# Copies with rows over 4096 bytes issued as two halves, and the first K load issued by ScalarE

## The chip, the cores and the metric

The kernel runs on one core of one Trainium2 chip. The metric is device time in microseconds (us) from a launch to its end. Three runs of the kernel before took 801.07, 794.12 and 801.41 us; the median is 801.07 us.

## The reference

Three stages follow one another, all in float32.

1. Attention with pooled queries: batch 2, 8 heads, 1152 positions, head size 64. Pairs of neighbouring queries are averaged, which leaves 576 per head and batch.
2. A mixture of experts over 1152 tokens of width 512: 8 experts, hidden width 1024, the two best experts of each token.
3. A dense layer with `h * cos(h)`: 512 to 2048 to 512.

```
q_pool = q.reshape(B, H, S // 2, 2, D).mean(axis=3)
scores = q_pool @ k.T / sqrt(D)
x = (softmax(scores) @ v)                       # heads side by side: [1152, 512]
noisy = x @ w_gate + log1p(exp(x @ w_noise)) * noise
out[token] += weight * (relu(x @ w1[e]) @ w2[e])   # for the token's two best e
h = x @ w_in;  result = (h * cos(h)) @ w_out
```

## The kernel before

**Number format.** Products need float32 accuracy, so each operand is split into a rounded high part and the rest. The scores of a head are `hi(q)*hi(k) + hi(q)*lo(k) + lo(q)*hi(k)`. With a head size of 64, two of the three products share one matmul of 128 rows. For that the operands are stacked on the partitions: the tile `q2` (named `q` in the trace) holds hi(q) twice, `l2` (`l`) holds lo(q) twice, `kt` holds hi(k) and lo(k), one above the other, and `kb` and `qd` serve the one query tile of each head that spans both batches.

**Attention.** Heads are worked in pairs: `hp` is the pair, 0 to 3, and `hl` the head in it. Each head has nine tiles of 128 queries, so there are 72 tiles. Tiles 0 to 3 of a head belong to batch 0, tile 4 to both, tiles 5 to 8 to batch 1. In each tile TensorE computes the scores of the next tile (L281), transposes the exponentials of this one (L321), and multiplies earlier ones with V (L359). VectorE takes the maxima, ScalarE the exponentials, GpSimd splits.

**Operands of a pair** are made while the pair before it is worked on. Their order is set by `plan` (L637): at each tile it lists which step is called, and the step's instructions stand in each engine's queue in that order. The steps are these.

- Q is loaded as 64 partitions per batch with 18 rows of 64 floats each: 4608 bytes of a partition are one contiguous row of the transfer (`load_q`, L85; for pair 0 `load_qb`, L197). Pair 1's loads go from SyncE's queue (SP), pairs 2 and 3 from ScalarE's.
- K is loaded likewise, 128 partitions per batch (`load_k`, L99). Its two heads are interleaved in SBUF, so its rows are 256 bytes long. Pair 0's K comes in three parts per batch and head.
- Q is pooled (L91, L202), transposed and split; K is transposed into `st` and split on GpSimd into `sh` and, in place, the low part in `st` (`k_split`, L227 and L228).
- The halves then have to change partitions, which copies from SBUF to SBUF do, all issued by SP, 64 partitions each: `q_asm` (L147, 4864 bytes per row), `l_asm` (L155, 4864), `k_asm` (L238 to L244, 4608, in the order ka high, KB 0, ka low, kb low, kb high, KB 1), and L752 for pair 0. `q_bd` (L163) copies 512-byte rows.

The score matmul of tile 4 of a pair's first head is the first that reads the `kt` of batch 1.

**The start.** SP issues Q of pair 0 and batch 0 for both heads (L680, L681), then K of batch 0 (six transfers), then Q and K of batch 1, V, and Q of pair 1. VectorE pools Q as soon as it lands (L202). ScalarE's first instruction is the load of its function table.

**Transfers and their marks.** Each transfer signals its landing on one of eight semaphores, which go round: an issue waits until the transfer eight before it has landed. SP and ScalarE share the eight.

**After attention** come the routing (L439), the gather of the experts' tokens, the experts (L967, L998) and the dense layer; their weights stream in over SP. The change touches none of that.

Of the kernel before, what the change touches and what calls it, by code (L numbers as in the profile page):

```python
# [9 lines left out]
F32 = mybir.dt.float32  # L10
# [12 lines left out]
def attn_moe_cos_kernel(ctx, tc, q, k, v, w_gate, w_noise, noise, w1, w2, w_in, w_out, out):  # L23
    nc = tc.nc
# [53 lines left out]
    QB1 = 640  # L78
    KT, Q2, QL, V2, QN, QP, KN, VN = {}, {}, {}, {}, {}, {}, {}, {}

    def load_q(hp, hl):
        t = prep.tile([128, 18, 64], F32, name="qn", bufs=2)
        QN[hp, hl] = t
        for b in range(B):
            (nc.sync if hp == 1 else nc.scalar).dma_start(t[b * 64:(b + 1) * 64], q[b, 2 * hp + hl].rearrange("(p r) d -> p r d", r=18))  # L85

    def pool_q(hp, hl):
        if hl == 0:
# [1 line left out]
        t = QN.pop((hp, hl)).rearrange("p (s r) d -> p s r d", r=2)  # L90
        (nc.gpsimd if hp else nc.vector).tensor_tensor(QP[hp][:, :, hl, :], t[:, :, 0, :], t[:, :, 1, :], op=OP.add)  # L91

    def load_k(hp, b, pool=None):
        t = (pool or prep).tile([128, 9, 2, 64], F32, name="kn", bufs=1)
        KN[hp, b] = t
        cs = [slice(0, 9)] if hp else [slice(3 * j, 3 * j + 3) for j in range(3)]
        for c in cs:
            for hl in range(2):
                nc.sync.dma_start(t[:, c, hl, :], k[b, 2 * hp + hl].rearrange("(p c) d -> p c d", c=9)[:, c])  # L99

    def load_v(hp, hl, b):
        t = qk.tile([128, 9, 64], F32, name="vn", bufs=2)
# [39 lines left out]
    def q_asm(hp, hl, bd=True):  # L142
        t = qk.tile([128, 1216], F32R, name="q2", bufs=3)
        QH = QS[hp]
        Q2[hp, hl] = t
        for s in range(2):
            nc.sync.dma_start(t.bitcast(F32)[s * 64:(s + 1) * 64], QH.bitcast(F32)[hl * 64:(hl + 1) * 64])  # L147
        if bd:
            l_asm(hp, hl)
            q_bd(hp, hl)  # L150

    def l_asm(hp, hl):
        t = QL2[hp, hl] = qk.tile([128, 1216], F32R, name="l2", bufs=2)
        for s in range(2):
            nc.sync.dma_start(t.bitcast(F32)[s * 64:(s + 1) * 64], QL[hp].bitcast(F32)[hl * 64:(hl + 1) * 64])  # L155

    KS, KB, QD, kbp = {}, {}, {}, []

    def q_bd(hp, hl):
        t = QD[hp, hl] = kbp[0].tile([128, 128], F32R, name="qd", bufs=2)  # L160
        for b in range(2):
            c0 = 4 * 128 if b == 0 else 4 * 128 - SQ + QB1
            nc.sync.dma_start(t.bitcast(F32)[b * 64:b * 64 + 64], QL[hp].bitcast(F32)[hl * 64:hl * 64 + 64, c0:c0 + 128])  # L163
# [30 lines left out]
    def load_qb(hl, b):  # L194
        if b == 0:
            QN[0, hl] = prep.tile([128, 18, 64], F32, name="qn", bufs=2)
        nc.sync.dma_start(QN[0, hl][b * 64:(b + 1) * 64], q[b, hl].rearrange("(p r) d -> p r d", r=18))  # L197

    def pool_qb(hl, b, eng):
        rs = slice(b * 64, b * 64 + 64)  # L200
# [30 lines left out]
    def k_asm(hp, b):  # L231
        h, r = KS.pop((hp, b))
        ka, kb = (qk.tile([128, S], F32R, name="kt", bufs=5) for _ in range(2))
        hf = h.bitcast(F32)
        if b == 0:
            k_stack(hp)
        rs = slice(b * 64, b * 64 + 64)
        nc.sync.dma_start(ka.bitcast(F32)[0:64], hf[0:64])  # L238
        if hp:
            nc.sync.dma_start(KB[hp, 0].bitcast(F32)[rs], hf[0:64])  # L240
        nc.sync.dma_start(ka.bitcast(F32)[64:128], r[0:64])
        nc.sync.dma_start(kb.bitcast(F32)[0:64], r[64:128])
        nc.sync.dma_start(kb.bitcast(F32)[64:128], hf[64:128])
        nc.sync.dma_start(KB[hp, 1].bitcast(F32)[rs], hf[64:128])  # L244
        KT[hp, 0, b], KT[hp, 1, b] = ka, kb

    def k_stack(hp):
        for hl in range(2):
            KB[hp, hl] = kbp[0].tile([128, S], F32R, name="kb", bufs=2)
# [387 lines left out]
    def plan():  # L637
# [5 lines left out]
        for hp in range(HP):  # L643
# [6 lines left out]
            if hp:  # L650
                m = n0 - 18
                if hp > 1:
                    at(m, load_q, hp, 0)
                    at(m + 1, load_q, hp, 1)
                d = 1 if hp == 1 else 0
                at(m + 1 + d, pool_q, hp, 0)
                at(m + 2 + d, pool_q, hp, 1)
                at(m + 2, load_k, hp, 0)
                for j in range(3):
                    at(m + (3 + 2 * d, 5 + d, 6 + d)[j], q_group, hp, j)  # L660
                at(m + 7 + d, q_split, hp)
                at(m + 8 + d, q_asm, hp, 0)
                at(m + 9 + d, q_asm, hp, 1, False)
                at(n0, l_asm, hp, 1)
                at(n0, q_bd, hp, 1)
                for j in range(3):
                    at(m + (8 + d, 9 + d, 10 + d)[j], k_group, hp, 0, j)
                at(m + 11 + d, k_split, hp, 0)
                at(m + 11 + d, load_k, hp, 1)
                at(m + 12 + d, k_asm, hp, 0)  # L670
                for j in range(3):
                    at(m + (14, 15, 16)[j], k_group, hp, 1, j)
                at(m + 17, k_split, hp, 1)
                at(m + 18, k_asm, hp, 1)
# [3 lines left out]
    pres = ExitStack()  # L678
    pro = pres.enter_context(tc.tile_pool(name="pro", bufs=1, side="right", reuse_waits="tile"))
    load_qb(0, 0)  # L680
    load_qb(1, 0)  # L681
    load_k(0, 0)
    load_qb(0, 1)
    load_qb(1, 1)
    load_k(0, 1, pro)
    warm(tbank, WQ)
    QP[0] = prep.tile([128, 9, 2, 64], F32, name="qp", bufs=1)
    QH = QS[0] = prep.tile([128, 1216], F32R, name="sh", bufs=2)
    QL[0] = prep.tile([128, 1216], F32R, name="ql", bufs=1)
    t = t0 = Q2[0, 0] = qk.tile([128, 1216], F32R, name="q2", bufs=3)  # L690
# [12 lines left out]
    c = slice(0, SQ)  # L703
# [11 lines left out]
    for n in sorted(e for e in ev if e < 0):  # L715
        for f, a in ev[n]:
            if f == load_v:
                f(*a)
    load_q(1, 0)
    load_q(1, 1)  # L720
    for i in range(3):
# [11 lines left out]
    c = slice(SQ, 1216)  # L733
# [4 lines left out]
    for j in range(3):  # L738
        k_group(0, 1, j)
    ev.setdefault(2, []).insert(0, (lambda: nc.scalar.activation(t0[64:128, c], QH[0:64, c], AF.Copy), ()))  # L740
    q_asm(0, 1, False)
    l_asm(0, 1)
    k_split(0, 1)
    for n in sorted(e for e in ev if e < 0):
# [4 lines left out]
    kbp.append(qes.enter_context(tc.tile_pool(name="kbp", bufs=1, reuse_waits="tile")))  # L749
    k_stack(0)  # L750
    k_asm(0, 1)
    nc.sync.dma_start(KB[0, 1].bitcast(F32)[0:64], KT[0, 1, 0].bitcast(F32)[64:128])  # L752
    q_bd(0, 1)
    load_gate()

# [4 lines left out]
    for n in range(NTOT):  # L760
        hp, hl, t = tiles[n]
# [427 lines left out]
    for e in range(E_N):  # L1189
        last = e == E_N - 1  # L1190
        for f in range(8):
            s = 8 * e + f
# [154 lines left out]
    for i in range(len(steps) + LAG):  # L1347
        if i < len(steps):
            b, f = steps[i]
# [14 lines left out]
        if i >= LAG:  # L1364
            b, f = steps[i - LAG]
# [126 lines left out]
```

## Time and profile before

| | |
|---|---|
| median of three runs | 801.07 us (794.12 to 801.41) |
| the profiled execution's own time | 799.73 us |
| its span, first to last instruction | 797.9 us |
| granted TensorE clock, mean over the span | 0.984 of full speed |
| TensorE matmul busy | 761.9 us (95%) |
| VectorE, ScalarE, GpSimd busy | 616.7, 514.5, 394.8 us |
| TensorE's share of the chain that ended last | 69% |

The profile shows one execution. A busy TensorE is not TensorE at its peak, since the ends of matmuls are modelled; the granted clock tells at which speed it ran. DMA shares are of the core's 16 DMA engines; a share slightly over 100% comes from packets that began in the stretch and ended behind it. A packet is one contiguous row of a transfer; packets of 4 bytes are the marks of landing, 16 per transfer. In the chain of waits each line tells a start, a length and what ran; "issue" is time without a wait that the profile shows.

### The profile page before, as it was taken

The page shows a single profiled execution, that of the slowest core. Times are in us where ns is not written, and L with a number is a line of the kernel's source. Part 1 is how long each engine was busy: PE and PEld are TensorE (multiplying, and loading weights), DVE is VectorE, ACT ScalarE, POOL GpSimd, SP SyncE. Part 2 cuts the span into 40 slices and gives each one's busy share as a digit, 9 for nine tenths or more (in the row PEclk, how much of TensorE's full clock was granted, in tenths as well). Part 3 has the DMA queues.
Part 4 walks back from the last instruction along what each step waited for, and adds up shares of the span by engine and source line. Part 5 has one row for each costly group of instructions (what it writes and reads, how often), then busy time and mean ns, then how long its engine had stood idle before and what let it go on. Part 6 is the DMA issues. An engine that isn't in the chain of part 4 may idle for free.

```text
span 797.9 us, 14088 instructions
## 1 busy us (share of the span) xinstructions
PE 761.9 (95%) x4979; PEld 703.4 (88%) x4979; DVE 616.7 (77%) x1225; ACT 514.5 (64%) x1224; POOL 394.8 (49%) x364
## 2 busy tenths in 40 slices
PE   7899999999999987899999999999988999999997
PEld 4699999989999977899899999999886989899996
DVE  5678778778888884479999999978678687685653
ACT  4789789879979862365555545556476566565553
POOL 3868767867868748106566665565156110100000
PEclk8999999999999999799999999999999999999999
DMA  9839679896873107487979889796634210100001
GB/s 207 174 81 209 148 183 230 215 253 136 221 176 115 60 18 256 155 291 253 318 255 346 270 287 335 241 337 217 233 90 128 75 33 27 35 20 27 2 1 42
DMA packets 91164, 133.67 MB, mean 168 GB/s; under 512 B 27952, under 2 KB 58032, under 8 KB 91088
## 3 DMA queue, kind: packets, MB, share of 16 engines
q1 hardware_dynamic: 84688, 111.21, 48.9%
q0 software_dynamic: 5392, 18.48, 6.4%
q10 hardware_dynamic: 1008, 3.02, 1.5%
q8 instruction: 41, 0.67, 0.4%
q14 instruction: 35, 0.29, 0.1%
HBM read 81.24 MB, written 29.88 MB: 139 GB/s over the span
## 4 chain that ended last, share of the span: by engine, by line
PE 69%; DVE 11%; DMA 6%; ACT 5%; issue 4%; POOL 3%; SPq 1%; ACTq 0%; DVEq 0%; POOLq 0%
PE h L967 20%; PE acc L967 11%; PE acc L998 8%; PE s L281 8%; PE pa L359 7%; PE pt L321 7%; DMA kt<-st 3%; DVE u L558 2%; PE pt L857 1%; ACT u L557 1%; PE t L959 1%; POOL st L228 1%; DVE hl L978 1%; PE t L1014 1%; DVE dw L1055 1%
## 5 line engine op out<-in xcount | busy, mean ns | idle before, releaser
L297 DVE TENSOR_REDUCE nm<-s 128x1 f32<-128x384 f32 x216 | 107.7, 549 | 34.8 <-PE s L281 22.1
L967 PE MATMUL h<-xe,u 128*128 128x320 f32 x768 | 129.0, 316 | 5.7 <-issue 5.6
L306 ACT ACTIVATE p<-s,nm 128x384 f32<-128x384 f32 x216 | 126.2, 593 | 1.5 <-DVE nm L299 0.5
L967 PEld LDWEIGHTS h<-xe,u 128*128 128x128 f32 x768 | 115.5, 190 | 9.5 <-issue 7.4
L1054 POOL TENSOR_SCALAR raw<-raw 128x1024 f32<-128x1024 f32 x16 | 65.9, 4119 | 104.3 <-ACT raw L1053 66.4
L558 DVE TENSOR_TENSOR u<-raw,u 128x1024 fp32r<-128x1024 f32 x66 | 88.8, 1349 | 16.9 <-ACT u L557 16.3
L321 PE MATMUL pt<-ident,p 128*128 128x128 f32 x645 | 95.0, 275 | 0.0
L281 PE MATMUL s<-kt,q 128*128 128x384 f32 x240 | 83.9, 371 | 6.8 <-DMA kt<-st 3.6
L967 PE MATMUL h<-x,u 128*128 128x256 f32 (+1 forms) x576 | 84.7, 296 | 4.5 <-DVE gl L1327 4.5
L967 PEld LDWEIGHTS h<-x,u 128*128 128x128 f32 x576 | 80.4, 189 | 9.2 <-DVE gl L1327 6.2
L359 PE MATMUL pa<-eh,v 128*128 128x320 f32 (+1 forms) x279 | 87.0, 326 | 0.0
L334 ACT ACTIVATE eh<-pt 128x384 fp32r<-128x384 f32 x144 | 63.1, 492 | 36.6 <-PE pt L321 34.5
L359 PE MATMUL pa<-el,v 128*128 128x320 f32 (+1 forms) x279 | 82.8, 310 | 0.0
L321 PEld LDWEIGHTS pt<-ident,p 128*128 128x128 f32 x645 | 77.7, 142 | 4.7 <-issue 1.8
L557 ACT ACTIVATE u<-raw 128x1024 fp32r<-128x1024 f32 x73 | 76.7, 1055 | 6.0 <-DMA raw<-w_d 4.8
L998 PE MATMUL acc<-hh,u 128*128 128x320 f32 x448 | 76.4, 313 | 0.0
L338 DVE TENSOR_TENSOR el<-pt,eh 128x384 fp32r<-128x384 f32 x144 | 73.2, 549 | 3.8 <-ACT eh L334 2.2
L345 POOL TENSOR_TENSOR el<-rw,eh 128x384 fp32r<-128x384 f32 x71 | 71.8, 1011 | 5.9
L998 PEld LDWEIGHTS acc<-hh,u 128*128 128x128 f32 x448 | 68.6, 190 | 0.4 <-ACT hh L977 0.3
L967 PE MATMUL acc<-u,gh 128*128 128x512 f32 x216 | 67.4, 393 | 0.0
L1072 POOL DMA_INDIRECT g<-y_d,ROWC x18 | 18.6, 1036 | 97.3 <-DVE cm L1080 67.1
L977 ACT ACTIVATE hh<-h 128x320 fp32r<-128x320 f32 x64 | 27.9, 435 | 55.7 <-PE h L967 40.6
(240 smaller groups left out, 1714.9 us busy)
## 6 DMA issues: line engine op xcount, KB each, us to landing
raw<-in_moe_w_dram SPq DMA_DIRECT2D x64, 512.0 KB, 5.5
raw<-in_moe_w_in_dram SPq DMA_DIRECT2D x16, 512.0 KB, 4.5
raw<-in_moe_w_out_dram SPq DMA_DIRECT2D x16, 512.0 KB, 6.6
w_d<-dw POOLq DMA_DIRECT2D x16, 512.0 KB
raw<-w_d SPq DMA_DIRECT2D x14, 512.0 KB, 4.3
xg_d<-ZERO SPq DMA_DIRECT2D x10, 512.0 KB, 3.9
vn<-in_v_dram SPq DMA_DIRECT2D x16, 288.0 KB, 4.8
q<-sh SPq DMA_DIRECT2D x14, 304.0 KB, 4.3
```

What stands on the lines that cost most here:

```text
L281: nc.tensor.matmul(o, l, r, start=(m == 0), stop=(not lo and m == len(mm) - 1))
L297: nc.vector.tensor_reduce(NM[n][:, i:i + 1], SB[n][i][:, 0:384], axis=AX.X, op=OP.max, negate=True)
L306: nc.scalar.activation(P[n][i], SB[n][i][:, 0:384], AF.Exp, bias=NM[n][:, 3:4], accum_out=SUMS[:, t, 2 * hp + hl, i:i + 1])
L321: nc.tensor.transpose(p[:, c], P[n][j][:, c], ident)
L338: nc.vector.tensor_tensor(el, t_src(n, j), ef, op=OP.subtract)
L345: nc.gpsimd.tensor_tensor(el, rw, ef, op=OP.subtract)
L359: nc.tensor.matmul(st["p"][:, 0:w], V2[hp, hl, b][:, c, :], (EH, EL)[s][:, c, EB[g]:EB[g] + w], start=(c == 0 and s == 0), stop=(c == 8 an ...
L557: nc.scalar.activation(b[:, 0], r, AF.Copy)
L558: st_w["lo"].tensor_tensor(b[:, 1], r, b.bitcast(F32)[:, 0], op=OP.subtract)
L967: nc.tensor.matmul(o, l, r, start=first and i == 0, stop=last and i == len(seq) - 1)
L998: nc.tensor.matmul(ACC[e, d][:, 0:CAP], w[:, i, 128 * d:128 * d + 128], r, start=f == 0 and r is hh and i == 0, stop=f == 7 and r is hl)
L1054: nc.gpsimd.tensor_scalar(m, m, 2.0 ** -15, 0.0, op0=OP.is_ge, op1=OP.add)
```

## The change

A helper `halves` issues a transfer as two, the first and the second half of each row. Every transfer with rows of 4608 or 4864 bytes goes through it, so rows become 2304 or 2432 bytes and the number of those transfers doubles. `load_k` takes an engine to issue from, and the first K load (pair 0, batch 0, six transfers of 256-byte rows) goes from ScalarE's queue.

```diff
+    def halves(eng, dst, src):
+        n = dst.shape[1] // 2
+        for c in (slice(0, n), slice(n, 2 * n)):
+            eng.dma_start(dst[:, c], src[:, c])
+
     def load_q(hp, hl):
...
-            (nc.sync if hp == 1 else nc.scalar).dma_start(t[b * 64:(b + 1) * 64], q[...])
+            halves(nc.sync if hp == 1 else nc.scalar, t[b * 64:(b + 1) * 64], q[...])
...
-    def load_k(hp, b, pool=None):
+    def load_k(hp, b, pool=None, eng=None):
...
-                nc.sync.dma_start(t[:, c, hl, :], k[...])
+                (eng or nc.sync).dma_start(t[:, c, hl, :], k[...])
...
     # q_asm, l_asm
         for s in range(2):
-            nc.sync.dma_start(t.bitcast(F32)[...], QH.bitcast(F32)[...])
+            halves(nc.sync, t.bitcast(F32)[...], QH.bitcast(F32)[...])
...
     # load_qb
-        nc.sync.dma_start(QN[0, hl][b * 64:(b + 1) * 64], q[...])
+        halves(nc.sync, QN[0, hl][b * 64:(b + 1) * 64], q[...])
...
     # k_asm
-        nc.sync.dma_start(ka.bitcast(F32)[0:64], hf[0:64])
+        halves(nc.sync, ka.bitcast(F32)[0:64], hf[0:64])
         if hp:
-            nc.sync.dma_start(KB[hp, 0].bitcast(F32)[rs], hf[0:64])
-        nc.sync.dma_start(ka.bitcast(F32)[64:128], r[0:64])
-        nc.sync.dma_start(kb.bitcast(F32)[0:64], r[64:128])
-        nc.sync.dma_start(kb.bitcast(F32)[64:128], hf[64:128])
-        nc.sync.dma_start(KB[hp, 1].bitcast(F32)[rs], hf[64:128])
+            halves(nc.sync, KB[hp, 0].bitcast(F32)[rs], hf[0:64])
+        halves(nc.sync, ka.bitcast(F32)[64:128], r[0:64])
+        halves(nc.sync, kb.bitcast(F32)[0:64], r[64:128])
+        halves(nc.sync, kb.bitcast(F32)[64:128], hf[64:128])
+        halves(nc.sync, KB[hp, 1].bitcast(F32)[rs], hf[64:128])
...
     load_qb(1, 0)
-    load_k(0, 0)
+    load_k(0, 0, eng=nc.scalar)
...
-    nc.sync.dma_start(KB[0, 1].bitcast(F32)[0:64], KT[0, 1, 0].bitcast(F32)[64:128])
+    halves(nc.sync, KB[0, 1].bitcast(F32)[0:64], KT[0, 1, 0].bitcast(F32)[64:128])
```

## Rows read from the trace of the kernel before

**Rows 1.** Chain that ended last, shares of the span, whole page.
```profile
PE 69%; DVE 11%; DMA 6%; ACT 5%; issue 4%; POOL 3%; SPq 1%; ACTq 0%; DVEq 0%; POOLq 0%
```

**Rows 2.** What TensorE's matmuls waited for: total, times, longest, in three stretches.
```profile
PE s L281 <- DMA kt<-st: 1.6, 1, 1.6
...
PE s L281 <- DMA kt<-st: 0.9, 1, 0.9
...
PE s L281 <- DMA kt<-st: 1.0, 1, 1.0
```

**Rows 3.** Chain of waits in order of time: start, length, what.
```profile
1.40 4.93 DMA qn<-in_q_dram
...
19.86 2.64 POOL st L228
...
22.51 7.70 DMA kt<-st
...
93.65 7.62 DMA kt<-st
...
160.31 7.71 DMA kt<-st
```

**Rows 4.** DMA packets and queue q1 in 21:25, 14:15 and 370:372 us.
```profile
DMA packets 240, 0.93 MB, mean 234 GB/s; under 512 B 48, under 2 KB 48, under 8 KB 240
...
q1 hardware_dynamic: 240, 0.93, 103.3%
...
DMA packets 187, 0.39 MB, mean 392 GB/s; under 512 B 20, under 2 KB 20, under 8 KB 187
...
q1 hardware_dynamic: 187, 0.39, 106.5%
...
DMA packets 212, 0.83 MB, mean 415 GB/s; under 512 B 2, under 2 KB 12, under 8 KB 212
```

**Rows 5.** SP's issues in order of time: start, length, line, transfer, count.
```profile
0.75 1.23 SPq L197 DMA_DIRECT2D qn<-in_q_dram  x2
...
15.81 1.14 SPq L147 DMA_DIRECT2D q<-sh  x2
...
88.48 1.11 SPq L155 DMA_DIRECT2D l<-ql  x2
89.64 2.61 SPq L163 DMA_DIRECT2D qd<-ql  x2
...
92.94 0.60 SPq L240 DMA_DIRECT2D kb<-sh  x1
...
94.89 1.87 SPq L242 DMA_DIRECT2D kt<-st  x1
```

**Rows 6.** Stretch, length, busy PE PEld DVE ACT POOL, clock, DMA share, GB/s.
```profile
28.00:30.00 2.00, 0.76 (x7) 0.50 (x5) 1.04 (x3) 1.93 (x7) 1.92 (x3) 1.00 1.05 240
...
32.00:34.00 2.00, 2.00 (x11) 1.54 (x10) 1.65 (x4) 0.20 (x1) 2.00 (x3) 0.59 0.91 166
34.00:36.00 2.00, 2.00 (x12) 2.00 (x12) 1.11 (x2) 1.85 (x7) 1.92 (x3) 0.56 0.25 21
...
10.00:20.00 10.00, 8.98 (x40) 6.95 (x40) 7.58 (x14) 6.41 (x22) 5.85 (x6) 0.66 1.12 242
```

**Rows 7.** Transfers by issue: count, size, median us to landing.
```profile
out_dram<-os SPq DMA_DIRECT2D x9, 256.0 KB, 2.0
...
kn<-in_k_dram SPq DMA_DIRECT2D x12, 96.0 KB, 4.7
```

**Rows 8.** ScalarE at the start and around its Q loads: start, length, idle before.
```profile
7.65 0.83 ACT L216 ACTIVATE sh<-pt 128x192 fp32r<-128x192 f32 x3 [5.62 <-PE pt L210]
...
88.85 0.87 ACT L334 ACTIVATE eh<-pt 128x384 fp32r<-128x384 f32 x2 [1.32 <-PE pt L321]
...
92.92 0.50 ACTq L85 DMA_DIRECT2D qn<-in_q_dram  x1
93.47 0.88 ACT L334 ACTIVATE eh<-pt 128x384 fp32r<-128x384 f32 x2 [1.63 <-PE pt L321]
```

More of the change, by code (lines that the diff above doesn't have):

```diff
@@ L84, in load_q @@
         for b in range(B):
-            (nc.sync if hp == 1 else nc.scalar).dma_start(t[b * 64:(b + 1) * 64], q[b, 2 * hp + hl].rearrange("(p r) d -> p r d", r=18))
+            halves(nc.sync if hp == 1 else nc.scalar, t[b * 64:(b + 1) * 64], q[b, 2 * hp + hl].rearrange("(p r) d -> p r d", r=18))
     def pool_q(hp, hl):
@@ L98, in load_k @@
             for hl in range(2):
-                nc.sync.dma_start(t[:, c, hl, :], k[b, 2 * hp + hl].rearrange("(p c) d -> p c d", c=9)[:, c])
+                (eng or nc.sync).dma_start(t[:, c, hl, :], k[b, 2 * hp + hl].rearrange("(p c) d -> p c d", c=9)[:, c])
     def load_v(hp, hl, b):
@@ L146, in q_asm @@
         for s in range(2):
-            nc.sync.dma_start(t.bitcast(F32)[s * 64:(s + 1) * 64], QH.bitcast(F32)[hl * 64:(hl + 1) * 64])
+            halves(nc.sync, t.bitcast(F32)[s * 64:(s + 1) * 64], QH.bitcast(F32)[hl * 64:(hl + 1) * 64])
         if bd:
@@ L154, in l_asm @@
         for s in range(2):
-            nc.sync.dma_start(t.bitcast(F32)[s * 64:(s + 1) * 64], QL[hp].bitcast(F32)[hl * 64:(hl + 1) * 64])
+            halves(nc.sync, t.bitcast(F32)[s * 64:(s + 1) * 64], QL[hp].bitcast(F32)[hl * 64:(hl + 1) * 64])
     KS, KB, QD, kbp = {}, {}, {}, []
@@ L196, in load_qb @@
             QN[0, hl] = prep.tile([128, 18, 64], F32, name="qn", bufs=2)
-        nc.sync.dma_start(QN[0, hl][b * 64:(b + 1) * 64], q[b, hl].rearrange("(p r) d -> p r d", r=18))
+        halves(nc.sync, QN[0, hl][b * 64:(b + 1) * 64], q[b, hl].rearrange("(p r) d -> p r d", r=18))
     def pool_qb(hl, b, eng):
```

## The prediction

> **What bounds the kernel now.** I read the chain of waits first. TensorE carries 69% of the span and DMA only 6% [rows 1], so a faster transfer is worth no more than the places where TensorE stands still for one. The waits of TensorE name three such places, all at a score matmul that needs the low part of K of batch 1: 1.6 us in 20 to 50 us, 0.9 in 50 to 110, 1.0 in 110 to 180 [rows 2]. The chain in order of time shows their origin: three copies `kt<-st` that take 7.6 to 7.7 us from issue to landing, and one Q load at the start that takes 4.93 us before anything can be pooled [rows 3]. Behind attention the chain has no transfer that the change touches.
>
> The DMA answers tell why a copy takes so long. In 21 to 25 us the 16 engines are full (103%) and move 234 GB/s: 240 packets less 48 marks are 192 rows of 4608 or 4864 bytes, and 4 us x 16 x 1.033 / 192 gives 344 ns for a row. In 14 to 15 us nearly all rows are V's, 2304 bytes long: the engines are as full, move 392 GB/s, and a row takes 16 us x 1.065 / 167 = 102 ns. In 370 to 372 us most packets are rows of exactly 4096 bytes: 415 GB/s [rows 4]. So rows of 4096 and of 2304 bytes go at one rate and rows just above 4096 at 0.6 of it. Two halves would cost 2 x 102 = 204 ns against 344.
>
> The Trainium skill (DMA: Bandwidth & Descriptors, section on bandwidth) gives a fixed 2.0 us plus the bytes over 436 GB/s, without a term for row length: an estimate from it is 2.7 us for a 288 KB transfer, and 4.7 for its two halves one behind the other, so that halving only adds. The rows of this trace differ with row length at equal load, and they decide here.
>
> **The change part by part.**
>
> *Halved copies, first K of batch 1.* The copy `kt<-st` is issued at 22.51, when GpSimd's split is through (19.86 + 2.64), and lands at 30.21 [rows 3]. It waits behind the backlog of Q loads and assemblies. The work ahead of it becomes 204/344 as long, so SP's issues become the limit: a copy costs SP 0.57 us (1.14 for two, from a moment without backlog), and with some 0.05 between them a half costs 0.62. From 15.81 [rows 5] there are 4 halves of q, 4 of l, 2 of ka high: 15.81 + 10 x 0.62 = 22.0, before GpSimd is through, so the second half of ka low goes out at 22.51 + 0.62 = 23.1. For its landing I have no row of a half. The shortest median in the list is 2.0 us, and 96 KB loads in the full queue of the start take 4.7 [rows 7]; I take 3.3, between them, since the engines are no longer full. It lands at 26.4, or 27.8 at the slow end; TensorE stands still only from 30.2 - 1.6 = 28.6. The wait goes whole: **1.6 us**. What is late next there is ScalarE, busy 1.93 of 2 us in 28 to 30 [rows 6], which is running already.
>
> *The clock behind it.* TensorE was busy 0.76 of 2 us in 28 to 30 at the full clock, and then the clock falls to means of 0.59 and 0.56 in 32 to 36 us, part of the time at the lower of the two levels, with TensorE busy all the time [rows 6]. That costs 2 x 0.41 + 2 x 0.44 = 1.7 us. With the stall gone the stretch ahead is fuller and I take the fall as gone: **1.7 us**; the bounds are 0 and 1.7.
>
> *The other two K assemblies.* Around 88 us SP issues l (2 copies), qd (2), ka high, KB 0 and then ka low; the landing at 93.65 + 7.62 = 101.27 ends a wait of 0.9. Halved, nine halves stand ahead of the last half of ka low: 88.48 + 9 x 0.62 = 94.1, and the two qd copies, 2.61 us now, in the backlog, and 1.14 without; I take 2.0. So it goes out at 96.1 and lands at 99.4 (98.1 to 100.8). TensorE needs it at 101.27 - 0.9 = 100.4: **0.9 us**, or at worst 0.5. The third place, 160.31, has the same shape and a wait of 1.0; I take **0.8**, as the margin is thin.
>
> *The first load.* VectorE starts on the second Q load, landed at 6.33 [rows 3]. Its last half goes out three issues after the first: two whole loads take SP 1.23 from 0.75 on [rows 5], so this is 0.75 + 3 x 0.62 = 2.6, and it lands 3.3 later, at 5.9; by the bounds of [rows 7] 4.6 to 7.3. Its rows pass faster; against that K now competes from ScalarE's queue at once, and no row shows this. Gain **0.5 us**, from -1.0 to +1.7.
>
> *K from ScalarE's queue.* Six issues of 0.57 are 3.4 us. ScalarE idles 5.62 us ahead of its first product at 7.65, waiting for TensorE's transposes of the pooled Q [rows 8], and that covers them. If the eight shared marks hold K's last issues until the first loads have landed, ScalarE may come up to 1 us late, which lies inside the bounds just given. SP is free some 3 us sooner for Q and K of batch 1; their users are not on the chain, so I count nothing. No row shows two queues side by side at the start.
>
> *Q loads from ScalarE* (pairs 2 and 3): eight more issues, 8 x 0.5 = 4 us of its queue, two halves more in each of four tiles. ScalarE idles 1.32 and 1.63 us there for TensorE's transposes [rows 8], which covers 1.0 per tile. If that cover is gone, exponentials come late and TensorE waits. The issue at 92.92 already came late, behind a mark of landing, so the bound is 2 us in all; I take 0, because marks come back sooner when transfers are shorter.
>
> *The remaining halves* (kb, KB, q) are wanted later than ka and only add to SP's queue; V and K loads behind them shift by 0.6 us per half, and SP's free time hides it.
>
> **The sum:** 1.6 + 1.7 + 0.9 + 0.8 + 0.5 = 5.5 us. The profiled execution took 799.73 us, so 794.2; it lies 1.3 us under the median of the runs, and carried over to that the sum gives 795.6. I put the forecast at 794.8.
>
> **The rivals.**
>
> *SP becomes the bound (slower).* L242 took SP 1.87 us and the two qd copies 1.3 each [rows 5]. I read that as waiting for a mark eight transfers back. If it is the price of an issue, a half costs 1.35 or so. Then ka low lands at 88.48 + 9 x 1.35 + 2.0 + 3.3 = 105.9, 4.6 later than now, and the third place, of the same shape, as much; at the first 15.81 + 11 x 1.35 + 3.3 = 34.0, 3.8 later. That is 13.0 us, less 0.5 for the first load: 812. It decides from 0.83 us per half on, gap included, where ka low lands at 101.27 as now. Against it: 1.11 and 1.14 for two copies, and 0.60 for KB 0 [rows 5]. Chance 0.07. The Trainium skill (DMA: Bandwidth & Descriptors, rules for kernel authors) has a rule for this side: gather small transfers into large ones.
>
> *Nothing changes.* No row shows a copy from SBUF to SBUF with rows of 2304 bytes; the fast rows come from or go to HBM. If the copies' rows take half of 344, the backlog stays and with it all three waits; Q loads alone gain 0.5: 799 to 800.5. Slow rows from HBM and slow rows from SBUF look alike in the trace, so I give it 0.15.
>
> *More than the waits.* The first 20 us run at a mean clock of 0.66 in their second half, with TensorE busy 8.98 of 10 us [rows 6]; a start without gaps would return up to 3.4 us. With 794.8 as a start, the first load's upper bound (1.2 more) and the same again for the clock come to 792, all of the 3.4 to 790. Chance 0.18.
>
> *Unrelated to the change:* the three runs of the kernel before span 7.3 us, more than the sum above. I take 2 to 3 us of noise on a median from it.
>
> **How the numbers follow.** My forecast has 0.60, with a range of its own of 791 to 799. The range for 8 in 10 takes in the larger gain and the unchanged case, 788 to 802, and leaves out the slow rival. A measurement of this kernel tells 1%, 8 us, from no change: faster means under 793.1. The forecast's lower end, a quarter of it, and the larger gain give 0.15 + 0.18 = 0.33 and a little from the noise, 0.35. Slower over 809: 0.07. Within 1%: 0.58.
>
> **What would show it.** Right: in the first 36 us, full DMA engines moving near 390 GB/s, or engines no longer full; `kt<-st` to landing under 5 us; no wait of TensorE on `kt<-st`; a full clock in 32 to 36 us; SP's issues at 0.5 to 0.6. Wrong: halves' rows near 170 ns; issues over 0.8 us; ScalarE's transposed copies late behind L85; the first pooling no sooner than before.

## The result, and the profile after

The changed kernel takes 804.98 us (median of 20 runs, 801.04 to 810.05); the kernel before, run beside it, takes 800.48 (20 runs, 794.12 to 803.75). The ratio is 1.007, 95% interval 1.0052 to 1.0088: some 5 us slower where 5.5 us of gain had been forecast. The profiled execution took 804.25 us, its span is 802.4 us.

*The copies.* DMA packets in 21:25 us of the changed kernel, as the first stretch of [rows 4]:

```profile
DMA packets 481, 0.93 MB, mean 233 GB/s; under 512 B 98, under 2 KB 98, under 8 KB 481
...
q1 hardware_dynamic: 481, 0.93, 104.1%
```

There are twice as many packets and the same bytes per second: 481 less 98 marks are 383 rows, and 4 us x 16 x 1.041 / 383 gives 174 ns for half a row. Two of them cost 348 ns, where a whole one cost 344. Halving bought no bandwidth.

*TensorE's waits.* Total, times, longest in the stretches 50:110 and 110:180 us, which answer to [rows 2]:

```profile
PE pt L612 <- DVE el L343: 2.8, 1, 2.8
...
PE pt L612 <- DVE el L343: 2.8, 1, 2.8
```

No wait on `kt<-st` is left. In their place are two longer ones, of the products with `GW` (L612) for a VectorE step of the exponentials (L343). The chain of waits in order of time (start, length, what) shows what the first was late for:

```profile
89.28 3.25 DMA x_d<-X
...
92.55 0.75 SPq L168
...
93.34 3.62 DMA qd<-ql
...
96.98 0.47 ACTq L84
...
97.50 0.50 ACT eh L339
...
98.02 0.57 DVE el L343
...
98.64 1.56 PE pt L612 x12
```

This is read from the bottom: TensorE's products at L612 wait for `el`, that for ScalarE's `eh`, and that for ScalarE's own issue of a Q half at 96.98 (`ACTq L84`). The issue went out only when SP's copy `qd<-ql`, under way from 93.34, had landed at 96.96. The two share no data, so what held it is the mark of landing that it takes over. The copy itself had been issued late, behind the landing of `x_d<-X`. ScalarE in order of time, where the bracket is idle time and what ended it:

```profile
95.68 1.77 ACTq L84 DMA_DIRECT2D qn<-in_q_dram  x2
97.50 0.87 ACT L339 ACTIVATE eh<-pt 128x384 fp32r<-128x384 f32 x2 [4.39 <-DMA qd<-ql]
```

The last of ScalarE's four Q loads was held in the kernel before too, at 92.92 [rows 8], but there no wait of TensorE followed.

*The clock.* Stretch, length, busy times, granted clock, DMA share, GB/s; the first two rows answer to [rows 6], and the last is 100 to 104 us of the kernel before:

```profile
10.00:20.00 10.00, 8.53 (x44) 6.82 (x43) 7.79 (x15) 7.39 (x23) 4.69 (x4) 0.50 1.14 247
...
32.00:36.00 4.00, 4.00 (x24) 2.92 (x23) 2.29 (x7) 2.52 (x9) 3.92 (x4) 1.00 0.54 106
...
100.00:104.00 4.00, 4.00 (x20) 3.90 (x20) 3.23 (x8) 1.78 (x5) 3.83 (x5) 0.57 1.06 221
168.00:172.00 4.00, 3.74 (x17) 3.74 (x18) 2.29 (x6) 2.07 (x8) 2.32 (x4) 0.60 1.05 222
...
100.00:104.00 4.00, 3.06 (x22) 2.77 (x21) 2.46 (x7) 1.43 (x5) 2.82 (x3) 1.00 1.02 218
```

The fall in 32 to 36 us is gone, but 10 to 20 us now run wholly at the lower level (1.2 GHz; mean 0.66 before). Behind each of the two waits at L612 TensorE runs at means of 0.57 and 0.60 for 4 us: a wait of 2.8 us comes with 1.7 and 1.6 us more, 4 x 0.43 and 4 x 0.40. Less the waits on `kt<-st` that are gone there, TensorE falls back by 2.8 us at the first place and by 3.0 at the second.

*The start.* Issues, VectorE's first poolings, and what SP's issues waited for in 0:9 us (total, times, longest):

```profile
0.75 7.53 SPq L84 DMA_DIRECT2D qn<-in_q_dram  x8
...
0.75 4.30 ACTq L104 DMA_DIRECT2D kn<-in_k_dram  x6
...
5.80 0.75 DVE L207 TENSOR_TENSOR qp<-qn 64x576 f32<-64x576 f32 x1 [3.55 <-DMA qn<-in_q_dram]
8.78 0.75 DVE L207 TENSOR_TENSOR qp<-qn 64x576 f32<-64x576 f32 x1 [2.22 <-DMA qn<-in_q_dram]
...
SPq L84 <- DMA kn<-in_k_dram: 2.9, 3, 1.2
```

The second pooling starts at 8.78, where its load had landed at 6.33 before [rows 3], and the first score matmul at 13.34 instead of 10.34. SP's Q issues stood still three times, 2.9 us in all, until K's transfers, issued by ScalarE, had landed: the fourth half, the last that the second pooling needs, went out at 3.84.

**Where the time went.** The same TensorE instruction starts later than in the trace of before by 3.0 us at the first score matmul, 1.3 from 45 to 92 us, 4.0 behind the first wait at L612, 7.0 behind the second, 7.3 at the end of attention and 4.5 at the end. Between attention and the end the kernel before has a low clock (0.50 in 319 to 329 us); this execution has 1.00 in 319 to 329 and 326 to 336, and a shorter fall later (0.52 in 343 to 350). The change touches nothing there.

### The profile page after: what moved, and what is told of

Same layout as the page of the kernel before. It is cut to its first block, busy times and chain, and to the rows that moved or that the text cites. A ratio compares the mean times of both kernels' runs of the same rounds, so it can differ in the third digit from the quotient of the medians.

```text
span 802.4 us, 14211 instructions
## 1 busy us (share of the span) xinstructions
PE 763.6 (95%) x4979; PEld 705.4 (88%) x4979; DVE 619.6 (77%) x1225; ACT 514.3 (64%) x1224; POOL 394.2 (49%) x364
## 4 chain that ended last, share of the span: by engine, by line
PE 68%; DVE 11%; DMA 8%; ACT 4%; issue 3%; POOL 3%; SPq 1%; ACTq 0%; DVEq 0%; POOLq 0%
PE h L972 17%; PE acc L972 11%; PE s L286 9%; PE pa L364 8%; PE pt L326 8%; PE acc L1003 6%; DVE u L563 2%; POOL xg_d L529 2%; DMA xr<-xg_d 2%; PE pt L612 2%; PE t L964 1%; ACT u L562 1%; PE pt L175 1%; DVE hl L983 1%; DMA qd<-ql 1%
## 5 line engine op out<-in xcount | busy, mean ns | idle before, releaser
L972 PE MATMUL h<-xe,u 128*128 128x320 f32 x768 | 126.0, 313 | 0.0
L563 DVE TENSOR_TENSOR u<-raw,u 128x1024 fp32r<-128x1024 f32 x66 | 90.8, 1380 | 17.6 <-ACT u L562 17.4
L286 PE MATMUL s<-kt,q 128*128 128x384 f32 x240 | 85.8, 380 | 2.3 <-ACT p L311 1.2
L343 DVE TENSOR_TENSOR el<-pt,eh 128x384 fp32r<-128x384 f32 x144 | 73.4, 549 | 9.6 <-ACT eh L339 7.7
L349 POOL TENSOR_SCALAR eh<-rw 128x384 fp32r<-128x384 f32 x71 | 36.5, 513 | 58.3 <-ACT rw L347 46.1
```

Of the source, the lines that this page charges most:

```text
L286: nc.tensor.matmul(o, l, r, start=(m == 0), stop=(not lo and m == len(mm) - 1))
L343: nc.vector.tensor_tensor(el, t_src(n, j), ef, op=OP.subtract)
L563: st_w["lo"].tensor_tensor(b[:, 1], r, b.bitcast(F32)[:, 0], op=OP.subtract)
L972: nc.tensor.matmul(o, l, r, start=first and i == 0, stop=last and i == len(seq) - 1)
```

## The experiments

Groups that were timed together ran on one chip and shared the runs of the kernel before. Each verdict is the ratio to those.

**1. The change taken apart** (before: 801.42 us).

*K alone.* Only the first K load moves to ScalarE's queue.

```diff
-    load_k(0, 0)
+    load_k(0, 0, eng=nc.scalar)
```

> The first K load alone goes from ScalarE's queue; no transfer is halved. Theory (two queues share the engines): K's rows now run beside Q's instead of behind them, so the second pooling on VectorE, which started at 6.35 us before and at 8.78 with the whole change, starts at 8 to 9, and the first score matmul comes 2 to 3 us later; the kernel is 2 to 4 us slower (803 to 804 against 800.5) and TensorE shows its three waits on kt<-st as before. Rival (the late start comes from the halved Q loads and their issues): the second pooling starts at 6.0 to 6.5 and the time is that of before.

797.46 us, ratio 0.9968 (0.992 to 1.0016). The second pooling starts at 7.87 and the first score matmul at 11.85, 1.5 us late, yet score matmul 50 is at 43.72 against 44.27: the landing of `kt<-st` (30.61) still ends that stretch, and swallows the later start. No loss is measured, so the expected one is refuted.

*SP's halves alone.* SP's transfers in halves, ScalarE's Q loads whole, K from SP.

```diff
+            if hp == 1:
+                halves(nc.sync, ...)
+            else:
+                nc.scalar.dma_start(...)
```

> All transfers that SP issues are halved; ScalarE's Q loads of pairs 2 and 3 stay whole and K stays with SP. Theory (ScalarE is held by marks of landing): no wait of 2.8 us ahead of the matmuls on GW near 100 and 168 us; rows of halved copies still take 160 to 170 ns; attention ends within 2 us of before, and the time is 799 to 802. Rival (SP's doubled issues are the cause): the two waits of about 2.8 us stay, time 804 or more.

797.83 us, ratio 0.9969 (0.993 to 1.0008): not told apart from the kernel before. The waits of 2.8 us are gone, as the theory has it (lines below).

*ScalarE's halves alone.* The same with the branches exchanged, and all of SP's transfers whole.

> Only ScalarE's Q loads of pairs 2 and 3 are halved, everything else as before. Theory (ScalarE is held by marks of landing): ScalarE's last halves of a pair wait for transfers issued before them, which are whole here and land later still; its transposed copies come late near 93 and 160 us and TensorE loses 2 to 4 us at each, time 803 to 807. Rival (SP's doubled issues are the cause): no new wait, time within 1 us of before.

803.19 us, ratio 1.0023 (0.9984 to 1.0063): by themselves not told apart from the kernel before either.

*All halves, K from SP.*

```diff
-    load_k(0, 0, eng=nc.scalar)
+    load_k(0, 0)
```

> All of the change except that the first K load stays with SP. Theory: the start is within 1.5 us of that of before (second pooling at 6.3 to 7.8), and the waits near 100 and 168 us stay at about 2.8 us each; time 802 to 804. Rival (halves make the start late): second pooling at 8 to 9 as with the whole change, time 805.

808.02 us, ratio 1.0058 (1.0012 to 1.0103): slower by itself. ScalarE's halves are the difference between this kernel and SP's halves alone, 0.9% of the time or some 7 us by the ratios. TensorE's waits in 14:46, 88:112 and 155:182 us, first with SP's halves alone:

```profile
PE s L290 <- DMA kt<-st: 0.2, 1, 0.2
...
PE pt L616 <- DVE el L347: 0.5, 1, 0.5
...
PE pt L616 <- DVE el L347: 0.3, 1, 0.3
```

with ScalarE's alone:

```profile
PE s L286 <- DMA kt<-st: 0.3, 1, 0.3
...
PE pt L612 <- DVE el L343: 1.6, 1, 1.6
...
PE pt L612 <- DVE el L343: 1.3, 1, 1.3
```

and with all halves:

```profile
PE s L286 <- DMA kt<-st: 1.3, 1, 1.3
...
PE pt L612 <- DVE el L343: 2.6, 1, 2.6
...
PE pt L612 <- DVE el L343: 3.1, 1, 3.1
```

The waits at L612 (L616 where the kernel is four lines longer) follow ScalarE's halves, and grow when SP issues halves beside them. The first line of each fence holds a warning. Up to some 84 us ScalarE's halves alone is the same program as the kernel before, and its wait on `kt<-st` is 0.3 us, not 1.6; SP's halves alone and all halves are one program up to there, with 0.2 and 1.3. That wait varies from execution to execution by as much as the prediction wanted to gain from it.

**2. Everything from SP, and the Q loads at other places** (before: 800.62 us).

*All halved, K and all Q loads from SP.*

```diff
-            halves(nc.sync if hp == 1 else nc.scalar, ...)
+            halves(nc.sync, ...)
```

> All transfers halved as in the change, K and all Q loads issued by SP; ScalarE issues no Q load. The number of transfers and of marks is that of the change. Theory (what costs is that ScalarE, which also makes the exponentials, stands behind a mark of landing): the two waits of 2.6 to 3.1 us ahead of the matmuls on GW vanish and the time is that of SP's halves alone, 796 to 800. Rival (twice the transfers in the round of eight marks slow everything): the waits stay, or the waits on kt<-st come back with 2 us or more, and the time is 803 or more.

818.49 us, ratio 1.0209 (1.0171 to 1.0247): my theory fell. ScalarE is free of issues now, but the eight Q halves stand behind twelve halves of the K assembly in SP's queue. TensorE's longest wait, SP's issue of these Q halves, and GpSimd's pooling:

```profile
PE pt L132 <- POOL qp L96: 18.3, 2, 9.2
...
101.96 3.29 SPq L84 DMA_DIRECT2D qn<-in_q_dram  x4
...
107.85 1.40 POOL L96 TENSOR_TENSOR qp<-qn 128x576 f32<-128x576 f32 x1 [12.85 <-DMA qn<-in_q_dram]
```

In the changed kernel ScalarE issued its first four halves from 87.25 on. This is the rival "SP becomes the bound", though by the count of issues at 0.6 us each and not by a dearer issue.

*Pair 1's Q loads behind the first K assembly*, nothing halved.

```diff
-    load_q(1, 0)
-    load_q(1, 1)
...
     k_asm(0, 1)
+    load_q(1, 0)
+    load_q(1, 1)
```

> The kernel before with one move: the Q loads of pair 1 are issued behind the first K assembly and not ahead of it. No transfer is halved. Theory (the copy of ka low waits behind a backlog of transfers onto half the partitions): with 4 of 14 transfers, some 5.4 us of DMA time, out of its way kt<-st lands near 26 us instead of 30.2, the wait of 1.6 us goes, and with it, where it fell, the lower clock behind it; 1.5 to 3.5 us faster, 797 to 799. Rival (the copy's own time is the bound): the wait stays within 0.3 us.

799.7 us, ratio 0.9989 (0.996 to 1.0017). `kt<-st` lands at 27.92 and the wait on it falls to 0.2; in 32 to 36 us the clock stays at 1.00, and from 37 to 140 us TensorE is 2.9 to 3.2 us ahead of the trace of before. At the end of attention 1.9 us of it are left, and no gain is measured at the end. The two later waits on `kt<-st` are 1.0 and 1.3.

*The same, and the low part of Q of each pair's second head three tiles later, the other Q loads one tile later.*

```diff
-                    at(m, load_q, hp, 0)
-                    at(m + 1, load_q, hp, 1)
-                d = 1 if hp == 1 else 0
+                    at(m + 1, load_q, hp, 0)
+                    at(m + 2, load_q, hp, 1)
+                d = 1
...
-                at(n0, l_asm, hp, 1)
-                at(n0, q_bd, hp, 1)
+                at(n0 + 3, l_asm, hp, 1)
+                at(n0 + 3, q_bd, hp, 1)
```

> As the run with pair 1's late Q loads, and in pairs 1 to 3 the copies l and qd of a pair's second head come three tiles later, and the Q loads of pairs 2 and 3 one tile later, so that the K assembly of batch 1 stands ahead of them. Theory (backlog): the waits on kt<-st of 0.9 and 1.0 us near 101 and 168 us go as well, 3.5 to 5.5 us faster than before, 795 to 797.5. Rival: the later Q loads make GpSimd's pooling late and give back 1 to 3 us at the next pair's first tiles, no faster than the run with the first move alone.

804.16 us, ratio 1.0042 (1.0016 to 1.0068). The waits on `kt<-st` are down to one of 0.2, but TensorE waits 4.9 us in two places for ScalarE's `st` (L321) and 2.0 for a K load: the steps pushed back are late themselves.

**3. What sets the rate of a row.** A kernel of transfers alone, one case after the other; it leaves out the reference's computation and writes zeros.

In the cut below `one(i)` is Q of one head, 64 rows, and `two(i)` that of two heads, 128 rows.

```
for i in range(4): nc.sync.dma_start(D[i], two(i))            # 128 partitions, rows of 4608 B
for i in range(4): nc.sync.dma_start(D[i][0:64], one(i))      # 64 partitions, rows of 4608 B
...                                                           # each also with rows of 2304 B
```

> Leaves out the whole computation and writes zeros; it only runs transfers, one kind after the other: from HBM to 128 partitions and to partitions 0 to 63, with rows of 4608 and 2304 bytes; the same within SBUF; partitions 0 to 63 and 64 to 127 by turns from one queue and from two; 32 partitions. Theory (partitions): full DMA engines move about 390 to 420 GB/s onto 128 partitions with rows of either length, about 180 ns for 4608 bytes and 93 for 2304, and 215 to 240 GB/s onto 64 partitions with rows of either length, 340 and 165 ns; two queues on the two halves come out above one. Rival (row length, the prediction's): 4608-byte rows take 340 ns on 128 partitions too, and 2304-byte rows 100 ns on 64.

Stretch, length, busy times, clock, DMA share, GB/s of one window in each case. From HBM: 128 partitions with rows of 4608 bytes, 64 with 4608, 64 with 2304, 128 with 2304. SBUF to SBUF: 64 with 4608, 64 with 2304, 128 with 4608. From HBM onto 64 low and 64 high partitions: from two queues, and by turns from one:

```profile
6.00:12.00 6.00, 0.78 (x8) 0.00 (x0) 1.00 1.02 418
18.00:22.00 4.00, 0.00 (x0) 0.00 (x0) 1.00 1.04 234
26.00:30.00 4.00, 0.00 (x0) 0.00 (x0) 1.00 0.83 230
35.00:39.00 4.00, 0.00 (x0) 0.00 (x0) 1.00 1.01 353
45.50:49.00 3.50, 0.00 (x0) 0.00 (x0) 1.00 0.97 195
53.00:57.00 4.00, 0.00 (x0) 0.00 (x0) 1.00 0.93 213
62.00:66.00 4.00, 0.00 (x0) 0.00 (x0) 1.00 1.02 409
71.00:77.00 6.00, 0.00 (x0) 0.00 (x0) 1.00 1.01 250
83.50:88.00 4.50, 0.00 (x0) 0.00 (x0) 1.00 0.99 229
```

The number of partitions decides: 353 to 418 GB/s on 128, 195 to 234 on 64, whatever the length of a row. The case of 32 partitions runs into the writing of the zeros and gives no window. The Trainium skill states this (SBUF — State Buffer, "Door 1: The DMA port swizzle"): partitions 0 to 63 reach 8 of the 16 ports, and the rate tends to some 218 GB/s against 436 for all 128. The runs agree on the half; the 234 of one window lies a little above that 218.

**4. The same inside the kernel, and ScalarE's share with K at its new place** (before: 796.38 us for the first three, 798.84 for the fourth).

*The change without ScalarE's halves.*

> The change without its halves on ScalarE's queue: SP's transfers in halves, the first K load from ScalarE's queue, ScalarE's Q loads of pairs 2 and 3 whole. Theory A (the loss sits in ScalarE's queue: its four Q loads near 90 us and near 165 us become eight issues, the last of which wait for marks of transfers eight places back and hold the products that VectorE and TensorE need): TensorE's two waits at L612 of 2.8 us are under 0.6 us each and the low clock right behind them is gone; the start is as in the change (second pooling near 8.8, first score matmul near 13.3), which is mostly absorbed by 44 us; 798 to 801. Theory B (halving costs wherever it is done, by more packets and more marks on SP): the waits at L612 stay over 1.5 us and the time stays at 804 to 806. Theory C (K beside Q at the start is the loss): the time stays at 803 or more although the waits at L612 are gone.

798.35 us, ratio 1.0021 (0.9995 to 1.0048); the two waits of 2.8 us are 0.5 and 0.4. The second pooling starts at 8.72, as in the change, so the late start alone does not cost 4 us.

*Each Q load of pairs 1 to 3 as one transfer onto 128 partitions.*

```diff
-        for b in range(B):
-            (...).dma_start(t[b * 64:(b + 1) * 64], q[b, 2 * hp + hl].rearrange("(p r) d -> p r d", r=18))
+        src = q[:, 2 * hp + hl].rearrange("b (p r) d -> b p (r d)", r=18)
+        (...).dma_start(t.rearrange("p r d -> p (r d)"), src)
```

> The kernel before, with each Q load of pairs 1 to 3 as one transfer onto all 128 partitions (rows of 4608 bytes as before) where there were two onto 64 partitions each; nothing is halved. Theory A (the number of partitions sets the rate, not the length of a row): in 16 to 24 us the engines move 300 GB/s or more instead of 230, the low part of K of batch 1 lands at 28 us or sooner instead of 30.2, TensorE's wait for it falls from 1.6 us to under 0.4, ScalarE issues two Q loads where it issued four, and the median is 796 to 799, that is 2 to 4 us under the kernel before. Theory B (rows above 4096 bytes are slow): 230 GB/s and 344 ns per row stay, the three waits stay at 1.6, 0.9 and 1.0 us, and the time is 800 to 801.

857.06 us, ratio 1.0766 (1.073 to 1.0802): neither theory. A window of the transfers, and TensorE's wait in 20:60 us:

```profile
36.00:40.00 4.00, 0.00 (x0) 0.00 (x0) 0.00 (x0) 0.00 (x0) 0.00 (x0) 0.50 0.13 53
...
PE s L281 <- DMA kt<-st: 20.7, 1, 20.7
```

0.13 of 16 engines is 2 engines. The source's outermost dimension is the batch, of size 2. The Trainium skill says so (DMA: Bandwidth & Descriptors, "Why a DMA increments its semaphore by 16 and not by 1"): the slowest dimension of both sides sets on how many engines a transfer is spread. The trace agrees.

*The same with SP's other transfers in halves.*

> The run before it in this list (each Q load of pairs 1 to 3 as one transfer onto 128 partitions) with SP's other transfers (first Q loads, copies of q and l, assembly of K) in two halves each; K from SP. Theory A (halving brings no rate and costs SP 0.6 us per extra issue): within 1.5 us of that run, 796 to 800; no wait of TensorE on the low part of K over 0.4 us in either. Theory B (the halves of SP's copies were worth some 3 us by themselves, as the run with SP's halves alone at 0.997 suggests): 2 us or more under that run, 793 to 796.

857.79 us, ratio 1.076 (1.0725 to 1.0795). The two engines decide here too; of halves it tells nothing.

*Q loads of two neighbouring heads of one batch onto 128 partitions in a single dimension.*

```diff
-        for b in range(B):
-            (...).dma_start(t[b * 64:(b + 1) * 64], q[b, 2 * hp + hl].rearrange("(p r) d -> p r d", r=18))
+        src = q[hl, 2 * hp:2 * hp + 2].rearrange("h (p r) d -> (h p) r d", r=18)
+        (nc.sync if hp == 1 else nc.scalar).dma_start(t, src)
```

> The kernel before with the Q loads of pairs 1 to 3 taken as two neighbouring heads of one batch onto 128 partitions in a single dimension (so the attention works on other rows of Q than the reference's, and the routing behind it differs; only the traffic up to the end of attention is read). Theory A (partitions set the rate): while these loads run, in 16 to 20 us, the engines move 330 GB/s or more, a row of 4608 bytes takes 200 ns or less, the low part of K of batch 1 lands at 28 us or sooner, and TensorE's first wait for it is under 0.4 us. Theory B (rows above 4096 bytes are slow): 230 GB/s, 344 ns per row, a landing at 30 us, a wait of 1.6 us.

Packets in 17:18 us, nearly all rows of these loads, and in 28:30 us, rows of the K assembly on 64 partitions:

```profile
DMA packets 92, 0.42 MB, mean 415 GB/s; under 512 B 2, under 2 KB 2, under 8 KB 92
...
q1 hardware_dynamic: 92, 0.42, 101.9%
...
DMA packets 116, 0.41 MB, mean 205 GB/s; under 512 B 27, under 2 KB 27, under 8 KB 116
...
q1 hardware_dynamic: 116, 0.41, 99.9%
```

90 rows of 4608 bytes take 16 us x 1.019 / 90 = 181 ns each on 128 partitions; 89 rows of about that length take 32 us x 0.999 / 89 = 359 ns on 64. Same kernel, same row length, half the time. The first come from HBM and the others from SBUF, which in experiment 3 made little difference (418 against 409 GB/s on 128, 234 against 195 on 64). TensorE waits nowhere on `kt<-st` in 14:46 us. Near 101 and 168 us it waits 2.9 and 1.7, longer than in the kernel before; why is open, so fast Q loads by themselves do not take those two away.

**5. ScalarE's issues three tiles earlier, where SP has little to issue** (before: 798.84 us).

```diff
-                    at(m, load_q, hp, 0)
-                    at(m + 1, load_q, hp, 1)
+                    at(m - 3, load_q, hp, 0)
+                    at(m - 2, load_q, hp, 1)
```

*In the whole change:*

> The change whole, with the Q loads of pairs 2 and 3 issued three tiles earlier (tiles 15 and 16 of the pair before, where SP has few issues), still eight halves on ScalarE's queue. Theory A (the halves wait for marks that SP's burst of copies holds): the two waits of TensorE at L612 of 2.8 us fall under 0.6 us, the low clock behind them goes, attention is 4 to 7 us shorter from its first score matmul than in the change (271.7), time 798 to 801. Theory B (eight issues cost ScalarE 4 us wherever they stand): waits of 1.5 us or more appear three tiles earlier, and the time stays at 803 to 806.

802.8 us, ratio 1.0053 (1.0023 to 1.0083). The waits at L612 are gone, and there are new ones three tiles earlier:

```profile
PE pt L175 <- DVE el L343: 4.7, 3, 2.7
```

So the issues cost by themselves: in the chain ScalarE's fill nearly all of 77.15 to 79.34 us, and only then comes `eh`.

*With SP's halves, ScalarE's loads whole, K from SP:*

> SP's transfers in halves, K from SP, ScalarE's Q loads of pairs 2 and 3 whole and three tiles earlier: the version that the runs point to. Theory A: the loads leave the stretch of the K assembly, so no wait on the low part of K and none at L612 over 0.4 us is left at 101 and 168 us; 2 to 4 us under the kernel before, ratio 0.995 to 0.9975. Theory B (earlier loads make GpSimd's pooling or the copies of that tile late instead): ratio 0.999 or more.

796.61 us, ratio 0.9983 (0.9957 to 1.0009).

*In the kernel before:*

> The kernel before with nothing but ScalarE's Q loads of pairs 2 and 3 three tiles earlier. If the place of the loads does it, TensorE's waits on the low part of K of 0.9 and 1.0 us at 101 and 168 us go and the time is 1 to 3 us under the kernel before; the first wait of 1.6 us stays. If the halves of SP's copies are what takes the waits away, the two stay at 0.5 us or more and the time is within 1 us of the kernel before; the run with SP's halves and early loads is then 2 us or more under this one.

797.42 us, ratio 0.9996 (0.9966 to 1.0026). Neither is told apart from the kernel before. In this one the waits on `kt<-st` near 101 and 168 us are gone although nothing is halved, as its first theory has it, and 2.0 us of waits on `el` stand three tiles earlier; the gain of 1 to 3 us does not show. With the start unchanged from it, the first wait on `kt<-st` is 2.6 us in this execution; with SP's halves on the same chip it is 2.5.

**6. Placing alone** (before: 801.42 us): pair 1's Q loads behind the first K assembly, the others three tiles earlier, nothing halved, K from SP.

> The kernel before with Q loads placed only: pair 1's behind the first K assembly, those of pairs 2 and 3 three tiles earlier; whole transfers, K from SP. Theory A (the waits are worth what the rows said, and come from Q loads standing in the way of K): first wait under 0.3 us and no low clock in 30 to 36 us, no wait on the low part of K at 101 and 168; attention's last score matmul 3 to 5 us sooner than in the kernel before (277.7), median 2 to 4 us under it, ratio 0.995 to 0.998. Theory B (ScalarE's queue and the routing behind attention take it back): attention ends 2 us sooner or less and the ratio is 0.998 to 1.001.

798.16 us, ratio 0.9961 (0.9935 to 0.9987): the one version of fourteen whose interval lies below 1. Of so many, one may do so by chance, so a gain of 0.4% is likely and not shown. No wait on `kt<-st` is left anywhere. Attention ends at 277.48, only 0.2 us sooner than in the trace of before: in this execution 13 to 26 us run at the low clock (0.50), and 2.2 us of waits on `el` stand where ScalarE's loads now are. The ratio met the first theory; its 3 to 5 us in attention did not show in this trace.

## Why the prediction was wrong

**The cause read from [rows 4] (failed).** "Rows of 4096 and of 2304 bytes go at one rate and rows just above 4096 at 0.6 of it." The stretches compared differed in two things. The rows of 4608 and 4864 bytes went to 64 partitions, V's rows to 128. The prediction even named the doubt, as the rival "nothing changes", but sought it in HBM against SBUF. Experiment 3 and the last kernel of experiment 4 settle it: 181 ns per row of 4608 bytes on 128, 359 on 64. The term 344 to 204 ns was in truth 344 to 348. (The formula that the prediction set aside stands in the Trainium skill, DMA: Bandwidth & Descriptors, "Anatomy of one DMA — SWDGE (gpsimd) path", as a fit to transfers that GpSimd issues; the copies here are SP's.)

**The waits on `kt<-st`, 1.6 + 0.9 + 0.8, and the clock, 1.7 (failed with it).** Where halves leave the start as it was, the first wait is 0.2, 1.3 and 2.5 us in three kernels; where nothing is halved there, 1.6, 0.3 and 2.6. That is no difference, and it shows that 1.6 was one draw. What halving does to the copy stands in the trace of SP's halves alone (GpSimd's split, SP's four halves of `kt<-st`, and the second of them from issue to landing):

```profile
19.88 2.63 POOL L237 TENSOR_TENSOR st<-st,sh 128x1152 f32<-128x1152 f32 x1
...
26.35 2.45 SPq L84 DMA_DIRECT2D kt<-st  x4
...
26.97 2.69 DMA kt<-st
```

The split is through at 22.51 as before, but the second half goes out at 26.97 and not at the 23.1 of the prediction, and lands at 29.66 and not at 26.4. With the engines as slow as before, part of the time that a whole copy spent in flight (7.70) is now spent in SP's queue. That no such wait stands in the trace of the change comes, at this first place, from TensorE being late itself. When the backlog in front of K really goes, by placing Q behind it, TensorE is 3.2 us ahead from 37 us on against the trace of before, and 0.4 in the kernel of experiment 6, where the low clock of the start lasts longer. So 1.6 + 1.7 = 3.3 may be a fair size, for a cause that the change does not remove.

The other two places are kinder to the prediction. Near 101 us the wait is 0.9 to 1.0 in three kernels with whole copies (before, K alone, pair 1's Q late), and none in the two with SP's halves and ScalarE's loads whole in their old place; near 168 us it is 1.0, 0.3 and 1.3 against none and 0.5. TensorE is not late there: 2 us ahead and 0.1 behind the trace of before at 91 us. New waits of 0.3 to 0.5 at L616 take part of it back. Another part has a cause that the prediction does not name. The change without ScalarE's halves near 168 us (two pieces of the chain, SP's issues):

```profile
161.90 5.84 DMA kt<-st
167.74 0.04 issue
167.78 1.76 PE s L290 x8
...
161.90 3.25 SPq L84 DMA_DIRECT2D kt<-st  x4
```

TensorE starts when the first of the four halves has landed: a score matmul reads 384 of 1152 columns, and the first half holds them. No gain of this is measured in the times, 0.9969 and 1.0021, whose intervals both take in 1.

**The first load, +0.5 within -1.0 to +1.7 (failed).** Halves alone gave the 0.4 (second pooling at 5.99 in two kernels, against 6.35). K from ScalarE's queue, running beside Q, cost 2.8 on top (8.78), and 1.5 where nothing is halved (7.87). There Q is issued when it was before, at 1.41, and takes longer, against 4.93 from 1.40 [rows 3]:

```profile
1.41 6.43 DMA qn<-in_q_dram
```

So K takes bandwidth from the loads that the first pooling waits for. In the change the marks come on top: the last half of Q goes out at 3.84, held by K's landing, and not at the 2.6 of the prediction. The prediction had covered ScalarE's 3.4 us of issues, rightly; it asked whether marks would hold K behind Q and not Q behind K, and left the shared engines to a bound that was too narrow. Most of it is swallowed later: K alone loses nothing that is measured.

**Q loads from ScalarE, taken at 0, bound 2 us (failed, and the largest loss).** The cover was read as 1.3 and 1.6 us of idle time per tile [rows 8] against 1.0 us of extra issues. But two issues more per load push `eh` back, and the last two wait for marks of copies that SP issued just before; with SP's transfers in halves too, the eight marks go round over half as many bytes. Measured: two waits of 2.8 us and 3.3 us of low clock behind them. Undone in the change, the ratio falls from 1.007 to 1.0021; added to SP's halves, it rises from 0.9969 to 1.0058. Experiment 5 shows that the issues count without SP's burst: there the halved loads still cost 4.7 us of waits on `el`, whole ones at the same place 1.0, 2.0 and 2.2 in three kernels.

**SP's issues at 0.62 us per half (the price right, the moment not).** In the change they lie near 0.60 where no mark is late: 1.24 for two copies of `kt<-sh` at 99.78. But the halves of q, counted from 15.81, start at 17.77 there.

**The rivals.** "Nothing changes" had the rate of the copies right and the time wrong, for it priced no cost on ScalarE. "SP becomes the bound" named the right kind of loss, a queue that is blocked by issues, on the wrong engine.

**The signs.** Three of the signs named for being right stand in the trace of the change: no wait on `kt<-st`, a full clock in 32 to 36 us, issues near 0.6. None of them belongs to the mechanism: TensorE is 1.3 to 3.6 us late in that stretch, and the issues cost what they cost before. What told was the row of a half, 174 ns, and ScalarE late behind its issues, both named as signs of being wrong.

What stays open: why the low clock behind attention comes and goes between executions, and how far ScalarE's loss in the change splits between marks and issue time, and what halves on SP's queue alone are worth.

## What to carry to other kernels

Before a rate is put down to one property of a transfer, compare transfers that differ in that property alone; here partitions and row length changed together. A transfer issued from a computing engine's queue costs that engine its issue and, if marks of landing are shared, the landing of what another queue issued before it. A stall of one or two microseconds read from a single execution is a draw: look at the same stretch in a second one before summing it. A sign that a kernel late for another reason would show too proves nothing.

## What the runs showed of the hardware

- Two transfers at once onto the lower and the upper 64 partitions do not add up: 250 GB/s from two queues, 229 by turns from one, against 418 for one transfer onto 128. The Trainium skill says the same (SBUF — State Buffer, "Can I just issue two DMAs to hit both halves?"), with 6% more for the pair than for a single one; here it is 250 against 234.
- One transfer with an outermost dimension of 2 moved 53 GB/s on 0.13 of the engines and held up all that stood behind it: 20.7 us for one wait.
- K in rows of 256 bytes beside Q stretched a Q load from 4.93 to 6.43 us, though it came from another queue.
- A transfer in two halves lets its reader start on the first: the score matmul of 167.78 ran with one half of `kt<-st` landed at 167.74, the others issued later.
